# Moving opening angles to ScalarE, row copies to VectorE, weight stores to another queue, and re-slotting V in a tuned FNet and gMLP kernel

## The chip, the cores and the metric

The kernel runs on one core of one Trainium2 chip. The metric is device time in microseconds (us), lower is better; each figure is a median over several executions. Profiled spans are some 1 to 2 us shorter than the timed figure of the same execution, and a profile is one execution, so I compare profiles with profiles and times with times.

## The reference, cut to what matters

```python
X = np.fft.fft(np.fft.fft(x, axis=1), axis=2).real      # x: (8, 3072, 256)
h = np.maximum(X @ w_in, 0.0)                           # w_in: (256, 1024)
u, v = h[..., :512], h[..., 512:]
v_n = (v - mean(v)) / np.sqrt(var(v) + 1e-6)            # over the 512 columns
v_s = np.einsum('ts,bsd->btd', w_spatial, v_n) + b_spatial[None, :, None]
out = (u * v_s) @ w_out                                 # w_spatial: (3072, 3072)
```

The costly part is the spatial product: a 3072 x 3072 matrix on 3072 x 512 values, eight times.

## The kernel before

TensorE does everything that is a product, in bf16. Each batch's spatial product is cut in four *chunks* (c = 0 to 3). I number the chunks of batch 0 as chunks 0 to 3 and those of batch 1 as 4 to 7. Batches 0 and 1 use a 2 x 2 block scheme of eight products ("classic"). Batches 2 to 7 use a seven-product scheme ("fast") on weight sums such as A11 + A12, formed once on VectorE during batch 1, and on sums of V blocks, formed at each batch's start.

While a chunk's products run, the work that prepares later chunks is dropped into *slots* between them: folding x (the symmetry step ahead of the transform), transforms, V of the next batch, u of the next chunk, output products and, in batch 0, the turning (transposing) of the weights.

```python
def fold_steps(b, j, home=XHOME):          # pair(0), pair(1), c, d, e, g
    def pair(h):
        def go():
            bk = fbank()
            for i in range(2):              # mirrored rows of x through TensorE
                mm(bk[...], rid[...], view(mt, ...), True, True)
            xa = ev(512 * h, [1, 512])      # x itself, in the home's fp32 half
            tt(DVE, ov(512 * h, [1, 512]), xa, bk, SUB)
            tt(DVE, xa, xa, bk, ADD)
        return go
    ...                                     # the rest folds in place, in xt and oto

# batch 0
for c in range(4):
    ...                                     # folds, V of batch 1, turned tiles
    fillers(sl, n, ns, ((), ((0, 0, 7), (1, 7, 14)), ((2, 0, 13),), ((3, 0, 13),))[c])
    ...
    classic_chunk(0, n, c, units, sl, c == 0)

# batch 1: 15 weight sums a chunk, in thirds of a tile
sums = [...]                                # tt(DVE, o, A.., A..), then GpSimd stores o
sl.spread(sums, 0.6, 15.5)
...
# batches 2 to 7
if c == 0:
    for i, k in enumerate((0, 1, 2, 4, 6)):
        sl.at[k].append(vsum[i])            # M3, M4, M1, M6, M7: sums of V blocks
fillers(sl, n, 14, ((c, 0, 13),))           # V of the next batch, class c
```

A line `(c, lo, hi)` for `fillers` says which class of V is made between which slots. In these traces an instruction that waits holds up what the program put behind it on the same engine.

## Time and profile before

| what | before |
|---|---|
| time, median of 3 runs | 1398.86 us (1395.82 to 1401.41) |
| span of the profiled run | 1394.5 us |
| V of batch 0 starts (here: the first weight product of batch 0) | 73.5 us |
| chunks 0, 1, 2, 3 | 52.5, 65.1, 53.9, 47.9 us |
| chunk 7 with the gap behind it | 52.0 us (41.7 of work, 10.3 of gap) |
| first chunk of batch 2; of batches 3 to 6 | 46.1; 42.7, 43.7, 42.6, 43.7 us |
| other chunks of batches 2 to 5 | 36.2 to 36.4 us |

The chunk lengths come from the trace: a chunk begins with the first of its weight products on TensorE and ends where the next begins. For chunk 0 my cut falls on the product before its first one, so every length of chunk 0 is 0.4 to 0.5 us too long. The way to read this table is to hold it against the 36.2 us of an undisturbed fast chunk. The first chunk of a batch does the same products and takes 6 to 7 us more. In batch 0 the chunks have different work, so each has to be compared with its own busy TensorE time. The lines that carry this are in the prediction.

### The profile page before, as it was taken

The page shows a single profiled execution, that of the slowest core. Times are in us where ns is not written, and L with a number is a line of the kernel's source. Part 1 is how long each engine was busy: PE and PEld are TensorE (multiplying, and loading weights), DVE is VectorE, ACT ScalarE, POOL GpSimd, SP SyncE. Part 2 cuts the span into 40 slices and gives each one's busy share as a digit, 9 for nine tenths or more (in the row PEclk, how much of TensorE's full clock was granted, in tenths as well). Part 3 has the DMA queues.
Part 4 walks back from the last instruction along what each step waited for, and adds up shares of the span by engine and source line. Part 5 has one row for each costly group of instructions (what it writes and reads, how often), then busy time and mean ns, then how long its engine had stood idle before and what let it go on. Part 6 is the DMA issues. An engine that isn't in the chain of part 4 may idle for free.

```text
span 1394.5 us, 20891 instructions
## 1 busy us (share of the span) xinstructions
PE 1260.9 (90%) x8056; PEld 770.9 (55%) x8056; DVE 772.1 (55%) x1538; ACT 671.3 (48%) x1489; POOL 315.2 (23%) x372
## 2 busy tenths in 40 slices
PE   1685778999999978999899989999899989999998
PEld 0343445665665535665566655665566646666665
DVE  8676333534577743667555564557466654446333
ACT  4481266754445524555555545555455545552111
POOL 6322222310222211222222211222122222222222
PEclk9999899999999989999999999999999999999999
DMA  8646668778777775888678886888688767778885
GB/s 152 140 90 162 161 167 188 182 197 319 287 261 291 288 268 212 287 295 285 231 261 289 289 270 227 284 284 286 232 283 285 275 212 275 275 268 288 305 296 203
DMA packets 100435, 343.53 MB, mean 246 GB/s; under 512 B 10692, under 2 KB 60400, under 8 KB 74736
## 3 DMA queue, kind: packets, MB, share of 16 engines
q1 hardware_dynamic: 49424, 267.48, 53.8%
q0 software_dynamic: 25312, 49.55, 16.3%
q10 hardware_dynamic: 25600, 25.17, 5.3%
q8 instruction: 63, 1.03, 0.3%
q14 instruction: 36, 0.29, 0.1%
HBM read 300.46 MB, written 67.66 MB: 264 GB/s over the span
## 4 chain that ended last, share of the span: by engine, by line
PE 74%; DVE 9%; DMA 6%; ACT 5%; issue 2%; POOL 2%; SPq 0%; ACTq 0%; DVEq 0%; POOLq 0%
PE bk L115 72%; DMA reg<-rawd 2%; DVE reg L154 2%; PE bk L600 2%; DVE u L154 1%; ACT junk L422 1%; DVE y L154 1%; DMA reg<-sumd 1%; DMA ovl<-in_moe_w_spatial_dram 1%; ACT reg L607 1%; ACT reg L438 1%; DVE oto L154 1%; DMA xmr<-in_x_dram 1%; DVE ovl L154 1%; DMA qt<-in_moe_b_spatial_dram 1%
## 5 line engine op out<-in xcount | busy, mean ns | idle before, releaser
L115 PE MATMUL bk<-reg 128*128 128x384 bf16 (+1 forms) x5576 | 996.9, 330 | 37.6 <-DVE reg L154 19.4
L115 PEld LDWEIGHTS <-reg 128*128 128x128 bf16 x5576 | 546.4, 99 | 430.8 <-issue 64.1
L154 POOL TENSOR_TENSOR p<-y,qt 128x384 f32<-128x384 f32 x48 | 63.0, 1313 | 559.3 <-DVE y L154 559.3
L552 ACT COPY ost<-bk 128x512 f32<-128x512 f32 (+1 forms) x128 | 61.1, 479 | 246.5 <-PE bk L115 230.8
L438 ACT ACTIVATE reg<-vt,sm 128x512 bf16<-128x512 f32 x168 | 127.5, 807 | 76.0 <-DVE sm L154 48.7
L154 DVE TENSOR_TENSOR u<-y,u 128x384 bf16<-128x384 f32 x256 | 145.4, 568 | 9.6
L422 ACT ACTIVATE junk<-vt,sm 128x512 bf16<-128x512 f32 x168 | 121.3, 722 | 39.0 <-DVE sm L416 24.2
L154 DVE TENSOR_TENSOR y<-bk,bias 128x384 f32<-128x384 f32 x160 | 88.5, 553 | 92.7 <-PE bk L115 91.7
L533 ACT ACTIVATE u<-bk 128x384 bf16<-128x384 f32 x128 | 61.8, 483 | 87.9 <-PE bk L115 87.9
L115 PE MATMUL bk<-wob,u 128*128 128x256 bf16 x768 | 100.5, 273 | 0.2 <-ACT ost L552 0.2
L154 DVE TENSOR_TENSOR qt<-qt,bk 128x384 f32<-128x384 f32 x48 | 26.6, 554 | 126.9 <-PE bk L115 126.9
L527 ACT ACTIVATE u<-bk 128x384 bf16<-128x384 f32 x128 | 61.0, 476 | 59.5 <-PE bk L115 59.5
L115 PEld LDWEIGHTS <-u 128*128 128x128 bf16 x768 | 75.1, 98 | 19.9 <-DVE u L154 0.4
L154 POOL TENSOR_TENSOR qt<-y,qt 128x384 f32<-128x384 f32 x48 | 62.6, 1304 | 73.9 <-DVE y L154 69.3
L416 DVE TENSOR_SCALAR sm<-sm 128x2 f32<-128x2 f32 x84 | 33.9, 404 | 78.3 <-ACT vt L414 78.0
L154 DVE TENSOR_TENSOR ovl<-reg 128x1536 bf16<-128x1536 bf16 x60 | 56.6, 952 | 21.1 <-DMA reg<-rawd 12.5
L401 ACT ACTIVATE vt<-bk 128x512 f32<-128x512 f32 x84 | 49.7, 592 | 37.1 <-PE bk L115 37.1
L154 DVE TENSOR_TENSOR qt<-bias,bk 128x384 f32<-128x384 f32 x48 | 26.6, 554 | 73.7 <-PE bk L115 73.7
L115 PE MATMUL bk<-B,w2d 128*128 128x384 bf16 (+1 forms) x128 | 42.7, 334 | 26.7 <-ACT u L527 26.7
L154 DVE TENSOR_TENSOR reg<-reg 128x3072 bf16<-128x3072 bf16 (+2 forms) x34 | 66.4, 1954 | 0.1
L583 POOL COPY reg<-ovl 128x1535 bf16<-128x1535 bf16 x21 | 32.0, 1523 | 150.0 <-DMA ovl<-in_moe_w_spatial_dram 150.0
L922 POOL DMA_DIRECT2D sumd<-ovl x60 | 32.5, 542 | 146.2 <-DVE ovl L154 133.9
(132 smaller groups left out, 1324.9 us busy)
## 6 DMA issues: line engine op xcount, KB each, us to landing
reg<-sumd SPq DMA_DIRECT2D x120, 1152.0 KB
reg<-rawd SPq DMA_DIRECT2D x64, 1152.0 KB
out_dram<-ost ACTq DMA_DIRECT2D x64, 384.0 KB
sumd<-ovl POOLq DMA_DIRECT2D x60, 384.0 KB, 4.0
rawd<-reg SPq DMA_DIRECT2D x16, 1152.0 KB
bias<-bprm SPq DMA_DIRECT2D x32, 576.0 KB
ovl<-in_moe_w_spatial_dram POOLq DMA_DIRECT2D x45, 384.0 KB, 6.1
xst<-in_x_dram SPq DMA_DIRECT2D x22, 512.0 KB
```

The source lines that it names most:

```text
L115: PE.matmul(o, lhsT=l, rhs=r, start=start, stop=stop, skip_group_check=True)
L154: eng.tensor_tensor(out=o, in0=a, in1=b_, op=op)
L401: ACT.activation(out=v, in_=bk, func=AF.Relu, accum_out=sm[:, 0:1])
L416: DVE.tensor_scalar(out=sm[:, 2:4], in0=sm[:, 0:2], scalar1=-1.0 / DH, scalar2=None, op0=MUL)
L422: ACT.activation(out=junk, in_=s["v%d" % i], func=AF.Square, bias=sm[:, 2 + i:3 + i], accum_out=sm[:, 4 + i:5 + i])
L438: ACT.activation(out=o, in_=view(v, 0, [[256, 2], [1, 256]]), func=AF.Identity, scale=sm[:, 6 + i:7 + i], bias=sm[:, 8 + i:9 + i])
L527: ACT.activation(out=u[:, jc, 0, :], in_=src, func=AF.Relu)
L533: ACT.activation(out=u[:, jc, 1, :], in_=src, func=AF.Relu)
L552: ACT.copy(out=s["o"][:, rs[0]:rs[0] + len(rs), :], in_=view(bk, 0, [[256, len(rs)], [1, 256]]))
L583: POOL.tensor_copy(out=view(reg, ro + 1, [[1, 1535]]), in_=view(st, so + 1535, [[-1, 1535]]))
L600: PE.transpose(bk[:, 128 * n:128 * n + 128], view(src, off, [[4, 128]]), idn)
L922: POOL.dma_start(out=sumd[c, mi][:, 1536 * r:1536 * r + 1536], in_=o)
```

## The change

The intent is to take waiting out of the opening, batch 0, the step from batch 1 to 2, and each batch's first chunk. The diff, cut to its core:

```diff
+    def turns_of(c):                       # opening angles: twelve of these
+            ACT.activation(out=o, in_=..., func=AF.Identity, scale=sc, bias=bi)
...
     def mirror_rows(i, stage=None):        # reversed row copies
-        POOL.tensor_copy(out=view(reg, ro + 1, [[1, 1535]]),
+        DVE.tensor_copy(out=view(reg, ro + 1, [[1, 1535]]),
                         in_=view(st, so + 1535, [[-1, 1535]]))
...
+    def after_turn(i):                     # rows loaded and mirrored ahead
+        mirror_rows(i + 2)
+        load_part(i + 4, 1)
+        load_part(i + 3, 0)
...
-                    SP.dma_start(out=rawd[tc_, 2 * th + i],
+                    ACT.dma_start(out=rawd[tc_, 2 * th + i],
...                                         # batch 0: folds and V over more slots
-            for j in range(3):             # chunk 0 had all three folds of batch 1
+            fold_of(1, 0, 0, 3)
+            fold_of(1, 1, 4, 8)
+        elif c == 1:
+            fold_of(1, 2, 0, 4)
+        elif c == 2:
+            fold_of(2, 0, 8, 14)
+        else:
+            fold_of(2, 1, 2, 8)
+            fold_of(2, 2, 9, 15)
-        fillers(..., ((), ((0, 0, 7), (1, 7, 14)), ((2, 0, 13),), ((3, 0, 13),))[c])
+        fillers(..., ((), ((0, 4, 14),), ((1, 0, 6.5), (2, 6.5, 14)), ((3, 0, 11),))[c])
...                                         # chunk 7: sums early, first loads early
-        sl.spread(sums, 0.6, 15.5)
+        sl.spread(sums, 0.6, 15.5 if c < 3 else 8.0)
+        if c == 3:
+            load_next()
+            sl.at[8].append(load_next)
...                                         # first chunk of batches 2 to 7
-                for i, k in enumerate((0, 1, 2, 4, 6)):
+                for i, k in enumerate((0, 1, 2, 3, 4)):
-            fillers(sl, n, 14, ((c, 0, 13),))
+            fillers(sl, n, 14, ((c, 1 if c == 0 else 0, 13.5 if c == 0 else 13),))
```

The rest of the diff reorders the opening (the width tables come after the last angle tables, the turned tiles ahead of the third fold) and moves a scratch area.

More of the change, by code (lines that the diff above doesn't have):

```diff
@@ L214 @@
     F_TAB, F_WID, H_XST, H_HIS, F_SPX, H_SPC, H_WI, H_CT = (
-        0, 5072, 12800, 18944, 12288, 46208, 43008, 45056)
+        0, 19200, 12800, 18944, 12288, 46208, 43008, 45056)
     def special_load():
@@ L248, in table_ramps @@
                   channel_multiplier=3, allow_small_or_imprecise_dtypes=True)
-    def tables(c):
-        kv = view(regf, F_TAB, [[1, 385]])
-        yy = view(regf, F_TAB + 416, [[1, 1155]])
-        ta = view(regf, F_TAB + 1584, [[1, 1155]])
-        fv = view(regf, F_TAB + 2752 + 1160 * (c % 2), [[1, 1155]])
-        if c == 0:
-            DVE.tensor_scalar(out=view(regf, F_TAB + 404, [[1, 3]]),
-                              in0=view(regf, F_TAB + 400, [[1, 3]]),
-                              scalar1=1.0 / 3072.0, scalar2=None, op0=MUL)
-        for j in range(3):
-            DVE.tensor_scalar(out=view(regf, F_TAB + 416 + 385 * j, [[1, 385]]), in0=kv,
-                              scalar1=float(FREQ[c]),
-                              scalar2=view(regf, F_TAB + 404 + j, [[1, 1]]),
-                              op0=ADD, op1=MUL)
+        for i, f in enumerate((1, 2, 3)):
+            DVE.tensor_scalar(out=view(regf, F_TAB + 400 + 3 * i, [[1, 3]]),
+                              in0=view(regf, F_TAB + 400, [[1, 3]]),
+                              scalar1=(1.0 / 3072.0 if i == 0 else float(f)), scalar2=None,
+                              op0=MUL)
+    def turns_of(c):
+        for j in range(3):
+            o = view(regf, F_TAB + 416 + 1160 * (c % 2) + 385 * j, [[1, 385]])
+            sc = view(regf, F_TAB + 400 + j, [[1, 1]])
+            f = FREQ[c]
+            bi = 0.0 if f == 0 else view(regf, F_TAB + 400 + 3 * (f - 1) + j, [[1, 1]])
+            ACT.activation(out=o, in_=view(regf, F_TAB, [[1, 385]]), func=AF.Identity,
+                           scale=sc, bias=bi)
+    def tables(c):
+        yy = view(regf, F_TAB + 416 + 1160 * (c % 2), [[1, 1155]])
+        ta = view(regf, F_TAB + 2736, [[1, 1155]])
+        fv = view(regf, F_TAB + 3896 + 1160 * (c % 2), [[1, 1155]])
         DVE.tensor_scalar(out=ta, in0=yy, scalar1=MAGIC, scalar2=None, op0=ADD)
@@ L568, in u_ap, with load_part, mirror_rows @@
         return view(reg, WOFF[k] + 128 * t, [[1536, 3], [1, 128]])
-    def load_rows(i, stage=(ovl, 0)):
+    HST = ((ovl, 0), (reg, 32256))
+    def load_part(i, hi, stage=None):
+        if i >= 24:
+            return
         c, h, r = i // 6, i % 6 // 3, i % 3
         row = (TROW[c][h] + 512 * r) * S
-        POOL.dma_start(out=view(ovl, 1536 + 1536 * (i % 3), [[1, 1536]]),
-                       in_=dram(moe_w_spatial, row, [[4 * S, P], [1, 1536]]))
-        POOL.dma_start(out=view(stage[0], stage[1], [[1, 1536]]),
-                       in_=dram(moe_w_spatial, row + 1536, [[4 * S, P], [1, 1536]]))
-    def mirror_rows(i, stage=(ovl, 0)):
-        ro = 29184 + 1536 * (i % 3)
-        st, so = stage
-        POOL.tensor_copy(out=view(reg, ro + 1, [[1, 1535]]),
-                         in_=view(st, so + 1535, [[-1, 1535]]))
-        POOL.tensor_copy(out=view(reg, ro, [[1, 1]]), in_=view(st, so, [[1, 1]]))
+        t, o = (stage or HST[i % 2]) if hi else (ovl, 1536 + 1536 * (i % 3))
+        POOL.dma_start(out=view(t, o, [[1, 1536]]),
+                       in_=dram(moe_w_spatial, row + 1536 * hi, [[4 * S, P], [1, 1536]]))
+    def mirror_rows(i, stage=None):
+        if i >= 24:
+            return
+        ro = 29184 + 1536 * (i % 2)
+        st, so = stage or HST[i % 2]
+        DVE.tensor_copy(out=view(reg, ro + 1, [[1, 1535]]),
+                        in_=view(st, so + 1535, [[-1, 1535]]))
+        DVE.tensor_copy(out=view(reg, ro, [[1, 1]]), in_=view(st, so, [[1, 1]]))
+    def after_turn(i):
+        mirror_rows(i + 2)
+        load_part(i + 4, 1)
+        load_part(i + 3, 0)
     def turn_steps(i, k0, k1, on_dve=(1,)):
         r = i % 3
-        wo, ro = 1536 + 1536 * (i % 3), 29184 + 1536 * (i % 3)
+        wo, ro = 1536 + 1536 * (i % 3), 29184 + 1536 * (i % 2)
         steps = []
@@ L648 @@
     prep_x(0, 0)
+    turns_of(0)
+    turns_of(1)
     POOL.iota(view(regf, F_WID + 920, [[1, P]]), pattern=[[1, P]], base=1 - P,
@@ L661 @@
     for i in range(3):
-        load_rows(i, stages[i])
+        load_part(i, 0)
+        load_part(i, 1, stages[i])
     tables(0)
     tables(1)
+    turns_of(2)
+    turns_of(3)
     special_rows()
+    POOL.iota(view(regf, F_WID + 1060, [[1, P]]), pattern=[[1, P]], base=0,
+              channel_multiplier=-1, allow_small_or_imprecise_dtypes=True)
+    POOL.tensor_scalar(out=idn, in0=view(regf, F_WID + 1060, [[1, P]]), scalar1=0.0,
+                       scalar2=None, op0=ALU.is_equal)
     for f in fold:
@@ L669 @@
         s()
-    POOL.iota(view(regf, F_WID + 1060, [[1, P]]), pattern=[[1, P]], base=0,
-              channel_multiplier=-1, allow_small_or_imprecise_dtypes=True)
-    POOL.tensor_scalar(out=idn, in0=view(regf, F_WID + 1060, [[1, P]]), scalar1=0.0,
-                       scalar2=None, op0=ALU.is_equal)
-    width_tables()
     tables(2)
     tables(3)
+    width_tables()
+    load_part(3, 1)
+    load_part(4, 1)
+    POOL.dma_start(out=wob, in_=dram(moe_w_out, 0, [[D, P], [P * D, 4], [1, D]]))
+    width_products()
     for s in fold_steps(0, 1, homes[1]):
         s()
-    width_products()
+    mirror_rows(0, stages[0])
+    mirror_rows(1, stages[1])
+    for i in range(3):
+        for s in turn_steps(i, 0, 1, ()):
+            s()
+        if i == 0:
+            mirror_rows(2, stages[2])
+            load_part(3, 0)
+        else:
+            after_turn(i)
+    for k in range(2):
+        ACT.dma_start(out=rawd[0, k], in_=view(reg, WOFF[k], [[1, 4608]]))
     for s in fold_steps(0, 2, homes[2]):
         s()
-    POOL.dma_start(out=wob, in_=dram(moe_w_out, 0, [[D, P], [P * D, 4], [1, D]]))
     bias_rows()
     prep_x(1, 0)
-    for i in range(3):
-        mirror_rows(i, stages[i])
-    turned = []
-    for i in range(3):
-        ts = turn_steps(i, 0, 1)
-        ts[-1] = (lambda g=ts[-1], i=i: (g(), load_rows(i + 3)))
-        if i < 2:
-            ts.append(lambda i=i: mirror_rows(i + 3))
-        turned += ts
-    turned.append(lambda: mirror_rows(5))
-    for k, s in enumerate(turned):
-        s()
-    for k in range(2):
-        SP.dma_start(out=rawd[0, k], in_=view(reg, WOFF[k], [[1, 4608]]))
     load_bias(0)
@@ L723 @@
         tsi = turn_steps(i, 2, 3)
-        tsi[-1] = (lambda g=tsi[-1], i=i: (g(), load_rows(i + 3), mirror_rows(i + 3)))
+        tsi[-1] = (lambda g=tsi[-1], i=i: (g(), after_turn(i)))
         ts += tsi
@@ L738 @@
     for k in (2, 3):
-        SP.dma_start(out=rawd[0, k], in_=view(reg, WOFF[k], [[1, 4608]]))
+        ACT.dma_start(out=rawd[0, k], in_=view(reg, WOFF[k], [[1, 4608]]))
     def classic_chunk(b, n, c, units, sl, done=False):
@@ L858, with fold_of @@
         sl = Slots(ns)
-        if c == 0:
-            for j in range(3):
-                fs = fold_steps(1, j)
-                if j < 2:
-                    fs[-1] = (lambda g=fs[-1], j=j: (g(), prep_x(1, j + 1)))
-                else:
-                    fs[-1] = (lambda g=fs[-1]: (g(), prep_x(2, 0)))
-                sl.spread(fs, 2.5 * j, 2.5 * j + 3)
-        else:
-            j = c - 1
-            fs = fold_steps(2, j)
-            fs[-1] = (lambda g=fs[-1], j=j: (g(), prep_x(2, j + 1) if j < 2 else prep_x(3, 0)))
-            sl.spread(fs, 6, 14)
-        fillers(sl, n, ns, ((), ((0, 0, 7), (1, 7, 14)), ((2, 0, 13),), ((3, 0, 13),))[c])
+        def fold_of(fb, j, lo, hi):
+            fs = fold_steps(fb, j)
+            nb, nj = (fb, j + 1) if j < 2 else (fb + 1, 0)
+            fs[-1] = (lambda g=fs[-1]: (g(), prep_x(nb, nj)))
+            sl.spread(fs, lo, hi)
+        if c == 0:
+            fold_of(1, 0, 0, 3)
[4 more added lines that the diff above has]
+            fold_of(2, 0, 8, 14)
+        else:
+            fold_of(2, 1, 2, 8)
+            fold_of(2, 2, 9, 15)
+        fillers(sl, n, ns, ((), ((0, 4, 14),), ((1, 0, 6.5), (2, 6.5, 14)), ((3, 0, 11),))[c])
         seq = ([(c, 1)] if c > 0 else []) + ([(c + 1, 0)] if c < 3 else [])
@@ L880 @@
                 ts = turn_steps(ti, ua, ub)
-                if ti + 3 < 24:
-                    ts[-1] = (lambda g=ts[-1], ti=ti: (g(), load_rows(ti + 3),
-                                                       mirror_rows(ti + 3)))
+                ts[-1] = (lambda g=ts[-1], ti=ti: (g(), after_turn(ti)))
                 st += ts
@@ L896, with load_next @@
         classic_chunk(0, n, c, units, sl, c == 0)
+    seq = [(b, c, mi) for b in range(2, B) for c in range(4) for mi in range(7)]
+    pos = [0]
+    def load_next():
+        if pos[0] < len(seq):
+            b, c, mi = seq[pos[0]]
+            wload((pos[0] + 1) % 3, c, ORDER[mi])
+            pos[0] += 1
     cur = [0, 1, 4, 2]
@@ L938 @@
             cur = nxt
-    seq = [(b, c, mi) for b in range(2, B) for c in range(4) for mi in range(7)]
-    pos = [0]
-    def load_next():
-        if pos[0] < len(seq):
-            b, c, mi = seq[pos[0]]
-            wload(pos[0] % 3, c, ORDER[mi])
-            pos[0] += 1
-    for _ in range(3):
-        load_next()
+    load_next()
     g = 0
@@ L973 @@
                 sl.at[7].insert(0, lambda n=n: load_bias(n + 1))
-            units = [(g + i) % 3 for i in range(7)]
+            units = [(g + i + 1) % 3 for i in range(7)]
             g += 7
```

## The prediction

> **What bounds the kernel now.** I read the page first: busy time by engine and the chain that ended last.
>
> ```profile
> PE 1260.9 (90%) x8056; PEld 770.9 (55%) x8056; DVE 772.1 (55%) x1538; ACT 671.3 (48%) x1489; POOL 315.2 (23%) x372
> ...
> PE 74%; DVE 9%; DMA 6%; ACT 5%; issue 2%; POOL 2%; SPq 0%; ACTq 0%; DVEq 0%; POOLq 0%
> ```
>
> TensorE carries the chain and no other engine is near full, so a gain can only come from TensorE's idle time: 1394.5 - 1260.9 = 133.6 us. The second view is a table of stretches that I cut at the kernel's own stages, found from where each chunk's first products start: V of batch 0, then the four chunks of batch 0, the gap between batches 1 and 2, and one later batch. The columns are length, busy time of PE, PEld, DVE, ACT and POOL, granted clock, DMA share and GB/s.
>
> ```profile
> 60.80:106.50 45.70, 36.83 (x252) 21.42 (x252) 30.04 (x90) 36.70 (x70) 10.71 (x16) 1.00 0.58 136
> 106.50:158.60 52.10, 28.55 (x192) 18.02 (x192) 26.66 (x56) 8.63 (x13) 10.85 (x14) 0.80 0.59 130
> 158.60:226.50 67.90, 56.78 (x429) 35.56 (x427) 28.85 (x69) 46.33 (x96) 18.68 (x27) 0.98 0.72 179
> 226.50:279.00 52.50, 49.60 (x398) 33.41 (x398) 20.49 (x46) 31.11 (x59) 13.33 (x20) 0.99 0.85 204
> 279.00:327.00 48.00, 45.16 (x327) 29.09 (x325) 18.17 (x43) 25.32 (x53) 6.56 (x9) 1.00 0.81 241
> 489.00:500.00 11.00, 0.66 (x3) 0.32 (x4) 2.67 (x4) 0.47 (x1) 1.28 (x3) 0.71 1.02 330
> 529.00:682.00 153.00, 148.28 (x912) 89.57 (x911) 90.76 (x180) 79.60 (x189) 31.59 (x29) 0.98 0.80 269
> ```
>
> The idle time sits in chunk 0 of batch 0 (23.6 us), chunk 1 (11.1), the gap (10.3), and some 4.7 us once in each later batch. The timeline tells the cause of each. In chunk 0 TensorE waits twice for the mirrored x rows of a fold:
>
> ```profile
> 119.16 0.75 POOL L149 DMA_DIRECT2D xmr<-in_x_dram  x1
> 125.20 0.61 PE L115 MATMUL bk<-xmr,rid 128*128 128x256 bf16 x2 [7.72 <-DMA xmr<-in_x_dram]
> 143.92 0.75 POOL L149 DMA_DIRECT2D xmr<-in_x_dram  x1
> 148.07 1.03 PE L115 MATMUL bk<-xmr,rid 128*128 128x256 bf16 x4 [11.19 <-DMA xmr<-in_x_dram]
> ```
>
> GpSimd issues those loads in its own order, behind a row copy that itself waits for a transfer. The waits show that this is the rule: 21 copies, 150 us.
>
> ```profile
> POOL reg L583 <- DMA ovl<-in_moe_w_spatial_dram: 150.0, 21, 12.4
> ```
>
> Before batch 2 the first summed weights are asked for only when batch 1 has ended, and TensorE stands until they land:
>
> ```profile
> 491.76 1.13 SPq L830 DMA_DIRECT2D reg<-sumd  x2
> ...
> 499.34 4.02 PE L115 MATMUL bk<-reg 128*128 128x384 bf16 x12 [10.40 <-DMA reg<-sumd]
> ```
>
> In the first chunk of a batch the fifth sum of V runs late on VectorE; ScalarE's normalised V of the next batch overwrites what that sum reads, so ScalarE waits, the u activation behind it waits, and TensorE with it:
>
> ```profile
> 676.46 2.55 DVE L154 TENSOR_TENSOR reg<-reg 128x3072 bf16<-128x3072 bf16 x1
> ...
> 679.04 1.52 ACT L438 ACTIVATE reg<-vt,sm 128x512 bf16<-128x512 f32 x2 [5.29 <-DVE reg L154]
> ...
> 681.56 0.48 PE L115 MATMUL bk<-B,w2d 128*128 128x384 bf16 x1 [4.41 <-ACT u L527]
> ...
> 681.83 3.59 PE L115 MATMUL bk<-reg 128*128 128x384 bf16 x12
> ```
>
> The same 4.41 us stands at 528.7, 833.1, 985.7 and 1137.0 us: five times, never in the last batch, which prepares no next V.
>
> [...] twelve products take 3.59 us after the wait and 2.11 us elsewhere. [...] the fold's 128x508 addition takes 0.69 us alone and 1.51 us beside the GpSimd copy.
>
> **The change, part by part.**
>
> *Angles on ScalarE.* Twelve VectorE multiplies of 385 elements (458 ns each, 5.5 us counted singly) become twelve ScalarE activations of about 0.5 to 0.7 us (estimate: a 385-wide ScalarE cast takes 0.48 us, and an activation with two per-partition operands costs more). At the start nothing comes of it: the first fold waits until 9.5 us for its rows anyway. Later tables 2 and 3 need 2 x (0.76 + 1.36) = 4.2 us of VectorE instead of 6.4. But the width tables now follow them, and GpSimd's ramps for these stand behind a memset that waits for ScalarE's sine of table 3: I place the width tables at 28 us, the width products at 31 to 37, the second fold (6.2 us) until about 42. The three turned tiles come before the third fold: nine ScalarE copies at 1.01 us plus the first latency, to about 53.5, and the third fold, 6.2 us, to about 60, where before it ended at 51.9 and the turning at 58.2. First transforms: 1 to 2 us later.
>
> *Copies on VectorE, three tiles ahead.* GpSimd loses 24 x (1.5 + 0.2) = 41 us and all its waits for landing; VectorE gains 24 x about 0.7 = 17 us [...]. In chunk 0 VectorE has 12.4 us for two folds, 8.8 for eight gates (0.55 + 0.56 each), 2 for turned copies, 2.1 for mirrors: 25 us. The mirrored x rows are issued early, as TensorE alone reads them. The other half of x still loads when the fold before has ended, some 5 us, now with one such wait inside chunk 0 because the third fold moves to chunk 1. TensorE's own work there is about 25 us at full clock. Chunk 0: about 28 us instead of 52.1.
>
> *V over more slots.* One V chunk (about 3.5 us of TensorE and 16 of ScalarE) leaves chunk 1, and chunk 2 takes one more. Chunk 1: 56.8 - 3.5 + 5 of waits for the third fold = 58.5 (was 67.9). Chunk 2: 49.6 + 3.5 + 7, as ScalarE there has 31 + 17 us to do = 60 (was 52.5). Chunk 3 gets a second fold: 48.5 (was 48.0). The four chunks: 195 instead of 220.5, so -25.5; with the opening -24.
>
> *Stores on ScalarE's queue.* 16 issues at about 0.4 us, off the path; the sync queue no longer stands behind them (86.9 us of waits), which no TensorE wait rests on. Zero.
>
> *First loads for batch 2, sums done by slot 8.* Saved: 10.4 us of standing, 1.9 on twelve products at half clock, 0.4 on transforms: 12.7. Given back: 15 sums at 0.95 us now meet folds, V and gates in eight slots (some 27 us of VectorE in 21), so chunk 7 may lose 3. Net -9.5.
>
> *V sums in slots 0 to 4, next V one slot later.* The last sum then starts at about 671.0 where the fourth did, ends at 673.6, and ScalarE first needs it after 677. VectorE's queue stays even: the fourth sum fits the 2 us before 669.9 when it waited for TensorE. Saved at each of five boundaries: 4.41 + 3.70 - 2.11 (cold against warm products) = 6.0; together -30.
>
> Sum: -24 - 9.5 - 30 = -63.5; 1398.9 - 63.5 = 1335, and I say 1336.
>
> **Rivals.** (a) *The waits in batch 0 only move.* For: the x load still follows the fold before, ScalarE has 48 us of work in chunk 2, and DMA is at 0.85 there. Against: DMA demand there is fixed at 0.85 x 52.5 = 45 us a chunk. Then only 5 of 24 us come: about 1355. (b) *The reversed copy is slow on VectorE.* [...] (c) *VectorE becomes the bound at the batch boundary* and the 4.41 us wait becomes one for a bank. For: five sums at 1.75 to 2.55 us in five slots of 2.45. Against: the count above. Half of the 30 lost: 1351. (d) *Better than I say:* the earlier stream also frees the opening, where GpSimd doubles VectorE's times, and chunk 2 stays near its TensorE time: 1322.
>
> **Range and chances.** The boundary and the gap, 40 us, are read from waits that repeat to 0.01 us; batch 0 carries the doubt, +-15. Predicted 1336, range 1318 to 1360. Faster by over 2% means below 1370.9, which the 40 us alone pass: 0.93. Within 2%: 0.06. Slower: 0.01.
>
> **What would show it.** Right: five waits of 4.41 us gone and a batch of about 147 us; no idle at the start of batch 2; chunk 0 below 32 us with no wait on mirrored x; the VectorE copy near 0.56 us. Wrong: a TensorE wait on ScalarE copies or VectorE in chunks 1 and 2 that restores their 120 us; first transforms later than 63 us; waits on summed weights in batch 2.

## The result, and the profile after

The changed kernel takes 1352.85 us (median of 4 runs, 1350.76 to 1354.26) beside 1397.34 us for the kernel before (median of 4). The ratio is 0.9676, with a 95% interval of 0.965 to 0.9703. A ratio, here and below, is the mean time of one kernel's runs over that of the other's of the same rounds, so it is not quite the ratio of the medians. Executions over 1.5% slower than the fastest of the same kernel are left out of the means.

It is faster by 3.2%, and 17 us above the point predicted. Most places that the prediction named changed, several of them not by the amounts given. First the page, busy time by engine and the chain that ended last:

```profile
PE 1248.3 (92%) x7995; PEld 767.5 (57%) x8056; DVE 765.6 (57%) x1573; ACT 682.4 (51%) x1505; POOL 271.7 (20%) x324
...
PE 72%; issue 9%; DVE 6%; ACT 5%; DMA 4%; POOL 2%; another core or an unknown queue 0%; ACTq 0%; POOLq 0%; DVEq 0%
```

TensorE's idle time fell from 133.6 to 1350.6 - 1248.3 = 102.3 us. Its busy time fell too, by 12.6 us, for the same work: fewer products ran cold, as I call the lower granted clock behind a wait (in the kernel before 0.50 over the 4.0 us behind the wait of 10.40 us, where twelve products took 4.02 us beside 2.11 elsewhere; over the whole span 0.978 before and 0.982 after), and the trace holds 61 products fewer, as some records can be missing. The views do not part the two. Now the same table of stretches, cut at the starts of this kernel's own stages: V of batch 0, chunks 0 to 3, chunk 7, and one batch from its second chunk to the next batch's first. The columns are those of the prediction's table.

```profile
60.80:106.40 45.60, 36.71 (x248) 21.51 (x252) 30.74 (x96) 36.66 (x70) 3.23 (x6) 0.98 0.45 108
106.40:134.10 27.70, 24.59 (x191) 16.28 (x189) 21.37 (x46) 8.56 (x13) 3.61 (x6) 0.94 0.87 214
134.10:198.50 64.40, 52.43 (x399) 34.13 (x399) 26.26 (x70) 30.97 (x60) 7.67 (x14) 0.92 0.78 194
198.50:264.80 66.30, 55.61 (x415) 36.11 (x417) 25.13 (x67) 43.52 (x92) 7.08 (x13) 0.95 0.71 176
264.80:315.90 51.10, 45.52 (x331) 29.27 (x332) 25.41 (x64) 28.13 (x56) 2.60 (x4) 1.00 0.59 201
437.50:490.80 53.30, 45.21 (x253) 26.28 (x253) 31.23 (x59) 19.91 (x47) 10.57 (x20) 0.90 0.80 288
527.40:672.70 145.30, 144.56 (x903) 88.35 (x910) 89.64 (x179) 79.39 (x189) 31.56 (x28) 1.00 0.83 283
```

The last line is the clean one: in a whole batch TensorE is idle for 0.7 us. About half of what is left lies where the change gained nothing: 43.6 us of idle TensorE ahead of 60.8 us, where the kernel before had 43.1, and 8.9 us in the first line, as before. The other losses sit in four lines. Chunk 1 has 12.0 us of idle TensorE, chunk 2 has 10.7, chunk 3 has 5.6 and chunk 7 has 8.1, and three of the four show a granted clock below 1.00. The granted clock is what to look at beside the idle time: the 12 us of chunk 1 cost more than 12, since the products after the long wait run slowly: over the 4.2 us behind it the granted clock is 0.50, and the first twelve weight products there take 3.45 us where 2.11 is usual.

| length in us | before | after | change |
|---|---|---|---|
| start of V of batch 0 | 73.5 | 73.8 | +0.3 |
| chunk 0 | 52.5 | 27.6 | -24.9 |
| chunk 1 | 65.1 | 64.5 | -0.6 |
| chunk 2 | 53.9 | 66.3 | +12.4 |
| chunk 3 | 47.9 | 51.1 | +3.2 |
| chunk 7 and the gap | 52.0 | 53.3 | +1.3 |
| first chunk of batch 2 | 46.1 | 36.5 | -9.6 |
| first chunks of batches 3 to 6 | 172.7 | 146.0 | -26.7 |

These add up to -44.6; the spans differ by 43.9. What TensorE waited for in chunks 1, 2 and 7 says where to look. The columns of the waits are the instruction that waited, what released it, us in total, times, and the longest. Chunk 1 of the kernel after:

```profile
PE bk L115 <- DVE xst L154: 9.8, 1, 9.8
```

Chunk 2 of the kernel after:

```profile
PE bk L115 <- ACT vt L407: 6.7, 3, 3.0
PE bk L616 <- ACT reg L623: 3.0, 1, 3.0
```

Chunk 7 of the kernel after:

```profile
PE bk L115 <- ACT u L533: 3.6, 1, 3.6
PE bk L115 <- DVE y L154: 2.3, 1, 2.3
PE bk L115 <- ACT vt L420: 1.3, 1, 1.3
```

The kernel before had no such waits in these chunks: in chunk 1 none for x beyond 0.7 us, in chunk 2 none over 1.2 us, in chunk 7 a single one of 1.0 us. Chunk 1's own waits of old, 10.1 us for turned copies, u and V, shrank to 1.4. After the 2.3 us in chunk 7 twelve products took 4.00 us where 2.11 is usual, at a granted clock of 0.50. Followed back in the timeline, the 9.8 us of chunk 1 end in a transfer. These lines, from three engines' timelines, have start, length, what was done, and in brackets the idle time ahead of it and what ended it:

```profile
135.35 0.81 ACTq L910 DMA_DIRECT2D rawd<-reg  x2
...
136.56 0.38 SPq L141 DMA_DIRECT2D xst<-in_x_dram  x1
...
147.75 0.69 DVE L154 TENSOR_TENSOR oto<-xst,bk 128x512 f32<-128x512 f32 x1 [10.29 <-DMA xst<-in_x_dram]
...
149.22 0.59 PE L115 MATMUL bk<-xmr,rid 128*128 128x256 bf16 x2 [9.79 <-DVE xst L154]
```

ScalarE's queue asks for the stores of two turned tiles (2 x 128 x 4608 x 2 bytes = 2.4 MB). Then 1.2 us later the sync queue asks for the x of the third fold (0.5 MB), which VectorE can use only 11.2 us after that. The prediction had put some 5 us there.

In the first chunk of batches 3 to 6 the wait of 4.41 us is gone; no wait of TensorE over 1 us is left between 527 and 690 us. The reversed copy on VectorE took 0.56 us:

```profile
42.18 0.56 DVE L594 COPY reg<-reg 128x1535 bf16<-128x1535 bf16 x1
```

### The profile page after: what moved, and what is told of

The parts are those of the page before. It is cut to its first block, busy times and chain, and to the rows that moved or that the text cites.

```text
span 1350.6 us, 20874 instructions
## 1 busy us (share of the span) xinstructions
PE 1248.3 (92%) x7995; PEld 767.5 (57%) x8056; DVE 765.6 (57%) x1573; ACT 682.4 (51%) x1505; POOL 271.7 (20%) x324
## 4 chain that ended last, share of the span: by engine, by line
PE 72%; issue 9%; DVE 6%; ACT 5%; DMA 4%; POOL 2%; another core or an unknown queue 0%; ACTq 0%; POOLq 0%; DVEq 0%
PE bk L115 70%; POOL sumd L953 2%; PE bk L616 2%; DMA reg<-sumd 1%; ACT junk L428 1%; DMA xst<-in_x_dram 1%; DMA xmr<-in_x_dram 1%; DVE xst L154 1%; DVE oto L154 1%; DVE u L154 1%; ACT reg L623 1%; DVE y L154 1%; DMA sumd<-ovl 0%; DVE ovl L154 0%; ACT reg L473 0%
## 5 line engine op out<-in xcount | busy, mean ns | idle before, releaser
L115 PE MATMUL bk<-reg 128*128 128x384 bf16 (+1 forms) x5576 | 988.4, 329 | 27.6 <-ACT reg L309 20.6
L558 ACT COPY ost<-bk 128x512 f32<-128x512 f32 (+1 forms) x128 | 61.1, 479 | 269.9 <-PE bk L115 248.0
L539 ACT ACTIVATE u<-bk 128x384 bf16<-128x384 f32 x128 | 61.6, 482 | 66.3 <-PE bk L115 66.2
L533 ACT ACTIVATE u<-bk 128x384 bf16<-128x384 f32 x128 | 61.1, 477 | 54.2 <-PE bk L115 54.2
L407 ACT ACTIVATE vt<-bk 128x512 f32<-128x512 f32 x84 | 49.7, 591 | 32.0 <-PE bk L115 31.9
L420 ACT ACTIVATE vt<-bk 128x512 f32<-128x512 f32 x84 | 49.1, 584 | 27.9 <-PE bk L115 27.9
L422 DVE TENSOR_SCALAR sm<-sm 128x2 f32<-128x2 f32 x84 | 32.4, 386 | 52.1 <-ACT vt L420 51.3
L154 POOL TENSOR_TENSOR p<-p,y 128x384 f32<-128x384 f32 x48 | 47.7, 995 | 59.3 <-DVE y L825 38.6
L623 ACT COPY reg<-bk 128x1024 bf16<-128x1024 bf16 x51 | 50.9, 1011 | 17.3 <-PE bk L616 17.1
```

The lines of the kernel that those rows point to most:

```text
L115: PE.matmul(o, lhsT=l, rhs=r, start=start, stop=stop, skip_group_check=True)
L154: eng.tensor_tensor(out=o, in0=a, in1=b_, op=op)
L407: ACT.activation(out=v, in_=bk, func=AF.Relu, accum_out=sm[:, 0:1])
L420: ACT.activation(out=v, in_=bk, func=AF.Relu, accum_out=sm[:, 1:2])
L422: DVE.tensor_scalar(out=sm[:, 2:4], in0=sm[:, 0:2], scalar1=-1.0 / DH, scalar2=None, op0=MUL)
L533: ACT.activation(out=u[:, jc, 0, :], in_=src, func=AF.Relu)
```

## The experiments

My theory after this reading had three parts. Chunk 7 loses what the early loads gain, as fifteen sums crowd VectorE's queue. Chunk 1 loses to the late x. Chunk 2 loses to ScalarE, which has two classes of V there. Rivals were that the early load itself delays chunk 7, and that batch 0 is bound by its transfers, so that waits only move. Twelve kernels ran; all gave the reference's result. Experiments 5, 6, 10 and 11 ran on another chip than the other eight. Each ratio is to the kernel before, and is to be held against the 0.9676 of the kernel after.

Chunk lengths come from one profile each. In the kernel after and in experiments 1, 2, 5, 6 and 9, which leave the chunks of batch 0 as they are, chunk 0 takes 26.0 to 27.8 us, chunk 1 63.9 to 64.5, chunk 2 66.2 to 68.3 and chunk 3 51.1 to 52.7, the four together 209.5 to 211. Differences of 2 us in one of these chunks are no finding.

### 1. Sums over the whole of chunk 7

```diff
-        sl.spread(sums, 0.6, 15.5 if c < 3 else 8.0)
+        sl.spread(sums, 0.6, 15.5)
-        for mi, (ka, kb, op) in (...):                  # order 2, 1, 0, 3, 4
+        for mi in (2, 1, 0, 3, 4) if c < 3 else (2, 4, 0, 1, 3):
```

> The kernel after, with the fifteen weight sums of chunk 7 (the last chunk of batch 1) spread over the whole chunk again, the two groups that read the tile which the second early load overwrites coming first; both early loads stay. Chunk 7 takes 53.3 us in the kernel after, and had 41.7 us of its own in the kernel before. Theory 'crowding' (fifteen sums in eight slots make gates and V statistics queue on VectorE): chunk 7 falls to 42 to 45 us and the time from 1352.9 to about 1343. Rival 'early load' (the 1.2 MB asked for at the start of chunk 7 share the transfer engines with the two tiles that the sums wait for): chunk 7 stays above 51 us, the time above 1350.

Measured: 1339.87 us, ratio 0.9591 (0.9577 to 0.9605). Chunk 7 takes 41.8 us, with the early loads in it and no gap behind it. Its line in the table of stretches:

```profile
437.70:479.50 41.80, 40.22 (x254) 24.77 (x254) 28.60 (x56) 19.92 (x47) 8.86 (x17) 1.00 0.91 335
```

The transfer share is higher than in the kernel after (0.91 against 0.80) and the chunk is 11.5 us shorter, with the clock back at 1.00. This speaks for crowding and against the early load. The order of the sums changed with their spread, because the second early load overwrites what two groups read; the run does not part the two.

### 2. Sums still crowded, no early loads

```diff
-        if c == 3:
-            load_next()
-            sl.at[8].append(load_next)
...
-    load_next()
+    for _ in range(3):
+        load_next()
```

> The kernel after with the sums still crowded into the first eight slots of chunk 7, but with all three first loads for batch 2 asked for after chunk 7, as before. Theory 'crowding': chunk 7's own work stays at 51 to 53 us and the gap of about 10 us before batch 2 comes back on top: about 1364. Rival 'early load': chunk 7's own work falls to 42 to 45 us and the gap comes back, so the two cancel: about 1353.

Measured: 1357.19 us, ratio 0.9716 (0.9701 to 0.973). Chunk 7 and the gap take 58.7 us, of which TensorE stands 5.9 us for the first summed weights, so the chunk's own work stays at 52.8. That is what crowding predicts. The gap that came back is smaller than the 10 us I expected:

```profile
PE bk L115 <- DMA reg<-sumd: 5.9, 1, 5.9
```

The loads were asked for at 489.2 us, as TensorE's last product ran. The kernel before asked 2.8 us after its chunk's end, because the request stood 2.7 us behind VectorE's last sum. So crowding costs the chunk 11 us with or without early loads. With crowded sums the early loads are worth 4 to 7 us (4 to 6 by the times, 7 by the chunks); with the sums spread, experiment 1 shows the whole gap of 10.3 us gone. They never needed the crowding.

What crowding means can be read from VectorE's own waits in chunk 7 of the kernel after:

```profile
DVE ovl L154 <- DMA reg<-rawd: 5.1, 1, 5.1
DVE ovl L154 <- DMA sumd<-ovl: 3.1, 3, 1.8
```

A sum stands for the load of a tile that it reads, and others for the stores of earlier sums. In the kernel before these waits were 2.2 us and nothing, in this experiment they are 5.4 and 1.1. So sums that come early wait for their data, early loads or not, and hold up the gates and statistics behind them.

### 3. The x of batch 1's third fold asked for early

```diff
+    XEARLY = ((regf, 9728), (reg, 21504))       # space that V of batch 1 takes later
+    prep_x(1, 2, XEARLY)                        # ahead of chunk 0
...
-            fs = fold_steps(fb, j)
+            fs = fold_steps(fb, j, XEARLY if (fb, j) == (1, 2) else XHOME)
...                                             # x of batch 2's first fold is asked for one fold earlier
```

> The kernel after, but the x rows of batch 1's third fold get a home of their own and are asked for at the start of chunk 0, not when the second fold has ended. In the kernel after chunk 1 takes 64.5 us and TensorE stands 9.8 us in it, as x takes 11 us to land behind the stores and tile loads. Theory 'late x' (that wait and the cold clock after it are chunk 1's loss): chunk 1 falls to 51 to 54 us, chunk 0 stays at 27 to 29, the time goes from 1352.9 to about 1341. Rival 'transfers at their limit' (the same bytes only compete elsewhere): chunk 1 stays above 60 us or chunk 0 or 2 grows by what it loses, and the time stays above 1349.

Measured: 1340.19 us, ratio 0.9598 (0.9582 to 0.9614). Chunk 0 takes 26.0 us, chunk 1 takes 52.1, chunk 2 takes 67.9. Chunk 1 in the table of stretches:

```profile
133.00:185.10 52.10, 49.73 (x399) 32.83 (x399) 26.21 (x70) 31.00 (x60) 6.36 (x12) 1.00 0.89 225
```

The same 399 products take 49.73 us of busy TensorE where they took 52.43, and idle time falls from 12.0 to 2.4 us. So chunk 1's loss was 9.6 us of waiting and 2.7 us of cold products (granted clock 0.92 over the chunk there, 1.00 here). The transfers run at a share of 0.89 and the waits do not reappear elsewhere: the four chunks together are 12.8 us shorter. So batch 0 was not at the limit of its transfers.

### 4. V of batch 1 spread from chunk 2 into chunk 3

```diff
-  ((1, 0, 6.5), (2, 6.5, 14)), ((3, 0, 11),)
+  ((1, 0, 8),), ((3, 4, 13),)       # class 2: chunk 2 slots 8 to 16, chunk 3 slots 0 to 4
```

> The kernel after, but the V work of batch 1 in chunk 2 is spread thinner: one class in slots 0 to 8, the first half of the next in slots 8 to 16, its second half in the first four slots of chunk 3, and the last class in slots 4 to 13 there (it was two classes in chunk 2 and one in chunk 3). Chunk 2 takes 66.3 us and chunk 3 51.1 in the kernel after. Theory 'ScalarE fills chunk 2' (43.5 us of its work in two long runs make TensorE wait for V and turned tiles): chunk 2 falls to 56 to 59 us, chunk 3 rises to 53 to 56, the time goes to about 1347. Rival 'folds and turned copies on VectorE, or transfers, bound chunk 2': chunks 2 and 3 together stay within 2 us of their 117.4 and so does the time.

Measured: 1357.02 us, ratio 0.9716 (0.9698 to 0.9733). Chunk 2 fell to 59.8 us, near what I expected, but chunk 3 rose to 63.7. It is a miss for both theories, and its trace says why. TensorE's longest wait in chunk 3 was for u:

```profile
PE bk L115 <- ACT u L539: 5.2, 1, 5.2
```

ScalarE's u activation stood behind a normalisation that needed a reciprocal from VectorE, and VectorE stood behind x:

```profile
299.45 0.69 DVE L154 TENSOR_TENSOR oto<-xst,bk 128x512 f32<-128x512 f32 x1 [8.03 <-DMA xst<-in_x_dram]
300.17 0.69 DVE L154 TENSOR_TENSOR xst<-xst,bk 128x512 f32<-128x512 f32 x1
300.77 0.16 DVE L435 RECIPROCAL sm<-sm 128x2 f32<-128x2 f32 x1
```

```profile
301.16 1.52 ACT L444 ACTIVATE reg<-vt,sm 128x512 bf16<-128x512 f32 x2 [5.46 <-DVE sm L154]
```

The reciprocal, 0.16 us of work, waited for an x load that it has nothing to do with. It is chunk 1's fault once more, in the chunk that has two folds: an x load asked for (at 290.97 us) in the chunk that needs it. In the kernel after VectorE's wait for this load was 3.6 us, and TensorE waited for nothing over 2.4 us in that chunk.

### 5 and 6. The batch boundary, one half at a time

Experiment 5 keeps the V sums in slots 0 to 4 and puts the next V back to slots 0 to 13:

```diff
-            fillers(sl, n, 14, ((c, 1 if c == 0 else 0, 13.5 if c == 0 else 13),))
+            fillers(sl, n, 14, ((c, 0, 13),))
```

> The kernel after, but with only one half of the batch-boundary part: the five sums of V stay in slots 0 to 4, and the next batch's V goes back to slots 0 to 13 (it was one slot later). First chunks of batches 3 to 6 take 36.5 us in the kernel after and 42.6 to 43.7 in the kernel before. Theory 'the last sum was late' (what counts is that it ends before ScalarE overwrites what it reads; it now ends some 5 us earlier): chunks stay at 36.5 to 37.5, time within 3 us of 1352.9. Rival 'both halves are needed' (ScalarE's first normalised V comes a slot sooner too and still meets the sum): 38.5 us or more each, 1363 or more.

Measured: 1358.73 us, ratio 0.9726 (0.9704 to 0.9748); the first chunks of batches 2 to 6 take 37.6 us each. Experiment 6 keeps V later and puts the sums back:

```diff
-                for i, k in enumerate((0, 1, 2, 3, 4)):
+                for i, k in enumerate((0, 1, 2, 4, 6)):
```

> The kernel after with only the other half: the next batch's V one slot later, the sums of V back in slots 0, 1, 2, 4 and 6. Theory 'the last sum was late': the wait of 4.41 us shrinks by one slot of some 2.45 us to about 2[...], so first chunks take 38 to 39.5 us and the time is 1361 to 1368. Rival 'the delay of V alone suffices': 36.5 us and 1353.

Measured: 1360.72 us, ratio 0.9747 (0.9723 to 0.977); these chunks take 38.2 us each. With batches 3 to 6 at 43.2 on average before and 36.5 after, the sums alone bring 5.6 of 6.7 us and the later V alone 5.0. They do not add because both shorten the same wait. TensorE's wait of 4.41 us in the kernel before brought cold products behind it (in batch 3 twelve took 3.59 us beside 2.11 elsewhere, and the granted clock was 0.57 over 3.8 us); either half alone makes it 0.9 or 1.4 us, and these chunks are 1.1 or 1.7 us longer than in the kernel after, so little is left for the other half. In the first chunk of batch 3, for experiment 5 and then for experiment 6:

```profile
PE bk L115 <- ACT u L533: 0.9, 1, 0.9
```

```profile
PE bk L115 <- ACT u L539: 1.4, 1, 1.4
```

Against what was expected, the chunks of experiment 5 lie just outside the theory's range (37.5) and its time is 5.9 us up, where 3 were allowed; five boundaries at 1.1 us account for it. Experiment 6 is as the theory has it in its chunks and 0.3 us under its range in time.

### 7. Stores back on the sync queue

```diff
-            ACT.dma_start(out=rawd[...], ...)    # in all three places
+            SP.dma_start(out=rawd[...], ...)
```

> The kernel after with the stores of turned weight back on the sync queue. The prediction: zero, so 1351 to 1355. Rival 'order of the queue': the x rows of a fold are asked for in the same slot just ahead of the stores, so on one queue they would go ahead of the 2.3 MB and land sooner than the 11 us of the kernel after: chunk 1 falls from 64.5 to 58 to 61 us and the time to 1347 to 1350. Rival 'the sync queue blocks': x loads and loads of summed weights wait behind stores that wait for turned copies: chunks 1 to 3 grow and the time passes 1357.

Measured: 1345.38 us, ratio 0.9619 (0.9599 to 0.9638). Chunk 1 takes 56.8 us instead of 64.5. The sync queue's and VectorE's timelines of this kernel:

```profile
137.09 0.38 SPq L141 DMA_DIRECT2D xst<-in_x_dram  x1
137.57 0.93 SPq L910 DMA_DIRECT2D rawd<-reg  x2
```

```profile
141.40 0.69 DVE L154 TENSOR_TENSOR oto<-xst,bk 128x512 f32<-128x512 f32 x1 [3.41 <-DMA xst<-in_x_dram]
```

Now x is asked for 0.5 us ahead of the stores, and VectorE can use it 4.3 us later instead of 11.2. So this part of the change was not free: it costs about 8 us by the ratios and 6.0 in the profiled spans (7.7 in chunk 1, with 2.9 given back in chunks 2 and 3). In chunk 1 it let the 2.4 MB be asked for first. Whether the one queue or only the earlier request makes x land sooner, this run does not tell apart.

### 8. Row copies back on GpSimd, rows still three tiles ahead

```diff
-        DVE.tensor_copy(out=view(reg, ro + 1, [[1, 1535]]), ...)
+        POOL.tensor_copy(out=view(reg, ro + 1, [[1, 1535]]), ...)
```

> The kernel after with the reversed row copies back on GpSimd, in the same place of the program, so with the rows still loaded three tiles ahead. Theory 'the look-ahead did it' (GpSimd's waits of 12.4 us each for landing rows held up the mirrored x loads; with rows loaded ahead they are gone, whoever copies): chunk 0 stays below 30 us and the time within 4 us of 1352.9. Rival 'the engine did it' (a copy of 1.5 us or more on GpSimd, its queue ahead of the x loads, and VectorE slowed beside it): chunk 0 above 33 us or chunks 1 to 3 longer by 10 us in sum, and 1363 or more.

Measured: 1357.98 us, ratio 0.9716 (0.9692 to 0.974). V of batch 0 starts 1.9 us earlier, chunk 0 takes 26.0 us, and chunks 1, 2 and 3 take 65.3, 70.8 and 54.2. A copy costs 1.50 us on GpSimd. So chunk 0 does not need VectorE for its gain: the look-ahead and the fold moved out of it are enough (these two I did not part). The four chunks together are 6 to 7 us longer than in the kernels with the same batch 0 (216.3 against 209.5 to 211), most of it in chunks 2 and 3, so the engine is worth that, less the 1.9 us that the opening gains by GpSimd. That VectorE's copy of 0.56 us feeds the turning sooner is the likely reason; it is not shown. Each theory has a part: by time, 5.1 us up, the first missed its 4 us and the rival's 1363 was not reached.

### 9. Opening angles back on VectorE

```diff
-            ACT.activation(out=o, in_=..., func=AF.Identity, scale=sc, bias=bi)
+            DVE.tensor_scalar(out=o, in0=..., scalar1=sc, scalar2=bi, op0=MUL, op1=ADD)
```

> The kernel after with the twelve opening angles back on VectorE (one multiply and add of 385 elements each), everything else as it is. The prediction gave the change of the opening +1 to +2 us in all and put none of it down as a gain of the angles: 1351 to 1353, V of batch 0 starting within 1 us of 73.8. Rival 'ScalarE took load off VectorE when it counts': V starts 2 to 5 us later, 1355 to 1358. Rival 'the angles cost more than they gave' (they bring a third table load of 1.28 us and about 0.6 us each on ScalarE): V starts 2 us or more earlier, 1350 or less.

Measured: 1351.92 us, ratio 0.967 (0.965 to 0.9691): the same time. In its profile V starts at 76.4 us, where the ten kernels with the opening of the kernel after, that one included, gave 73.4 to 75.2, so the angles may be worth 1 to 3 us of the opening. The time shows none of it; chunk 0 is 1.6 us shorter here, but it takes either 26.0 or 27.3 to 27.8 us from run to run in kernels that do not touch it. The third table load that one rival counts is there: the kernel after loads ScalarE's tables at 0.75, 5.49 and 66.14 us, 1.28 us each, the kernel before at 0.74 and 65.80. I leave this part as "no measurable effect".

### 10. A version with 1 and 3, and one fold to a chunk

```diff
+        elif c == 1: fold_of(1, 2, 0, 4); fold_of(2, 0, 8, 14)
+        elif c == 2: fold_of(2, 1, 8, 14)
+        else:        fold_of(2, 2, 7, 14)
```

> A version meant to beat both: sums of chunk 7 spread over the chunk and x of batch 1's third fold asked for early, as in the two runs that measured 13 us and 12.7 us less; and as the x loads are now a chunk ahead, the folds of batch 2 stand one in each of chunks 1, 2 and 3 (they were one in chunk 2 and two in chunk 3), so that no x load is asked for in the chunk that needs it. If the two gains add: 1352.9 - 13.0 - 12.7 = 1327.2, and chunk 3 with one fold less takes 48 to 50 us where it had 51: 1325. Rival 'one gain hides the other or chunk 1 pays for its second fold': chunk 1 above 55 us, time above 1330.

Measured: 1327.03 us, ratio 0.9504 (0.9483 to 0.9526). Chunk 1 takes 53.2, chunk 2 takes 67.6, chunk 3 takes 48.9 and chunk 7 takes 41.6. The two gains add (1327.2 was the sum). The folds of batch 2 were moved in the same run; what that move is worth (2 us less in chunk 3, 1 more in chunk 1) lies within the spread of one profile, and it was not run by itself.

### 11. The same with V of batch 1 spread evenly

```diff
-  ((0, 4, 14),), ((1, 0, 6.5), (2, 6.5, 14)), ((3, 0, 11),)
+  ((0, 4, 11),), ((2, 4, 14),), ((3, 0, 11),)   # class 1: chunk 1 from slot 11, chunk 2 to slot 4
```

> The same version with V of batch 1 spread evenly: the second class in slots 11 to 16 of chunk 1 and 0 to 4 of chunk 2, the third in slots 4 to 14 of chunk 2 (chunk 2 had both). Theory 'two V classes on ScalarE make chunk 2 long' (TensorE waits there 10.1 us for ScalarE): chunk 2 falls from about 67 to 58 to 60 us and chunk 1 rises from 52 to 55 to 57, the time by about 5 us to 1320. Rival 'V costs the same wherever it stands': the two chunks together unchanged, and 1325.

Measured: 1325.9 us, ratio 0.9495 (0.9475 to 0.9514). Chunks 1 and 2 take 60.8 and 60.4 us, in sum 121.2 where they took 120.8: the rival's case, but for chunk 3, which is 2.5 us shorter. V on ScalarE costs the two chunks the same in these two placements, and the time (0.9495 against 0.9504) does not tell the versions apart. The waits of chunk 2 changed their name, from V to turned tiles:

```profile
PE bk L616 <- ACT reg L623: 6.1, 3, 2.6
```

### 12. The same with two of three turned copies on VectorE

```diff
-                ts = turn_steps(ti, ua, ub)
+                ts = turn_steps(ti, ua, ub, (0, 2))
```

> The even version (1325.9) with two of the three turned copies of each tile on VectorE and one on ScalarE in chunks 0 to 3 (it was the reverse). One costs 0.69 us on VectorE and 1.01 on ScalarE. Theory 'ScalarE is what chunk 2 waits for' (6.1 us of TensorE's waits there are for ScalarE's turned copies): chunk 2 falls from 60.4 to 55 to 57, chunk 1 from 60.8 to 58 to 60, the time to 1318 to 1321. Rival 'the wait changes its name': TensorE waits as long for VectorE's copies, 1325 or more.

Measured: 1322.77 us, ratio 0.9458 (0.9433 to 0.9482). Chunk 2 falls from 60.4 to 54.4 us and ScalarE's busy time there from 40.9 to 35.4; chunk 1 stays at 60.9. What TensorE waits for in chunk 2 is now spread thin, and its longest two waits are:

```profile
PE bk L115 <- ACT u L539: 1.6, 1, 1.6
PE bk L616 <- DVE reg L621: 1.2, 2, 0.9
```

So in chunk 2 it was ScalarE's load, not V as such. Chunk 1 did not follow, and the time is 1.8 us above the range expected. Nearly all of the gain is given back in this profile: chunk 0 takes 1.9 us more, and the third chunk of batch 1 takes 44.2 us where it took 41.2, with one wait of 2.3 us for u, behind a normalisation that waits 3.4 us for VectorE. That is why the profiled spans of experiments 11 and 12 (1321.6 and 1321.0 us) hardly differ and the intervals of their ratios touch; the gain in time is not shown. Both beat the kernel after clearly, by about 2% of the time before.

## Why the prediction was right or wrong

The class and the range were right: 1352.85 lies within 1318 to 1360, and the direction was never in doubt. The point was 17 us low. By its own steps, with the chunk lengths of the profiled runs:

- **Opening, +1 to +2.** Measured +0.3 at the start of V. Right in kind: no gain from the angles, which experiment 9 bears out. An activation took 0.67 us in the mean (0.60 to 0.61 for the three with one per-partition operand, 0.69 for the nine with two), within the 0.5 to 0.7 estimated. The places given inside it held: the second fold ended at 42.2 us (about 42 predicted) and the third at 58.4 (about 60).
- **Reversed copy, near 0.56 us.** Measured 0.545 to 0.565 us over 24 copies, and 0.15 for the one element copied behind each, 0.71 for the pair where about 0.7 was counted; on GpSimd the copy takes 1.50 us (experiment 8). The 0.56 was my estimate; no trace of the kernel before could show it, as that kernel has no such copy on VectorE. Rival (b) is out. One reading beside it was wrong: the addition of 1.51 us, which takes 0.69 elsewhere, ended at 45.24 us and GpSimd's copy began at 45.26, so it ran beside GpSimd's requests for transfers. The operations that did run beside the copies were slower too: one of 128x256 took 1.68 us there and 0.42 elsewhere.
- **Chunk 0, about 28 us.** Measured 27.6. The reason was right as well, and experiment 8 narrows it: chunk 0 is as short with GpSimd copying, so it was not the change of engine that freed the mirrored x loads.
- **Chunk 1, 58.5 us.** Measured 64.5; wrong by 6. The prediction's table ends chunk 1 at 226.5 us, where chunk 2's first product ran at 223.6, so the 67.9 and 56.8 that it starts from were 65.1 and 54.3 (and its terms add to 58.3). Started rightly the sum is 55.8, and the miss 8.7. The step that failed is "some 5 us" for the load of x. Behind the stores of this very change it took 11.2; TensorE stood 12.0 us in the chunk, and the wait brought 2.7 us of cold products (granted clock 0.92 in the chunk). Experiment 3 removes the wait: 52.1.
- **Stores, "Zero".** Wrong. The text asked whether a wait of TensorE rested on the *sync* queue's waits, and none did; it did not ask what the stores would be in front of on their new queue. Experiment 7 gives about 8 us back by undoing this part, and chunk 1 falls by 7.7: it is the miss of chunk 1 once more.
- **Chunk 2, 60 us.** Measured 66.3; wrong by 6. Cut at its own first products, the chunk before had 50.6 us of busy TensorE and not 49.6, which makes the sum 61.1. The rest is two terms: busy time came to 55.6 where 54.1 was counted, and 7 us for ScalarE's load was too little, as idle time is 10.7, 10.1 of it waits for ScalarE. The mechanism, ScalarE overfull in chunk 2, was right (experiment 12).
- **Chunk 3, 48.5 us.** Measured 51.1; it has two folds and an x load between them. With one fold it takes 48.9 (experiment 10).
- **Chunk 7 gives back 3 us.** The largest miss by the figures as given: it gave back 11.6 (53.3 against 41.7 us). The step counted VectorE's busy time, "some 27 us of VectorE in 21", and took the small excess for the whole cost. But the queue runs in order (0.16 us of work stood behind a wait of 8.03 us in experiment 4), and the early sums themselves waited for transfers (8.2 us where it was 2.2): gates and V's statistics stood behind sums, ScalarE behind the statistics, TensorE behind ScalarE, and the granted clock was 0.90 over the chunk. Experiment 1 takes all of it away without giving up the early loads.
- **Gap, 12.7 us saved.** The gap is gone, as predicted, and with it the cold products behind it (twelve took 4.02 us at a granted clock of 0.50). Experiment 2 adds what the step did not see: part of the old gap was a request that stood behind the last sum, and with the sums done early the gap is 5.9 us even without early loads.
- **Boundaries, 5 x 6.0 = 30 us.** Right (the sum's 3.70 for twelve cold products is no line of the trace; five groups took 3.44 to 4.05): four of them gave 26.7, or 6.7 each, and the fifth is in the -9.6 of batch 2's first chunk. The account of the cause, the last sum ending too late, held too, though experiments 5 and 6 show that either half of the edit would have brought five sixths or three quarters of it.

Of the rivals, (a) was half right: waits in batch 0 moved, from chunk 0 to chunks 1 and 2. It gave 1355 as the time, close to what came, but its reason, that too little would be gained in batch 0, was only part of it. Over chunks 0 to 3 the gain was 9.9 us, not 5, and the remaining miss lay in chunk 7. Batch 0 was also not bound by its transfers, as experiment 3 shows. (c) did not come: VectorE became no bound at the boundary. (d) did not come either, but the faster versions pass it by hand: 1322.77 us.

What stays open: experiment 12's loss in batch 1, and whether stores on the sync queue would still help the versions that ask for x early. These combinations were not run.

## What to carry to other kernels

A sum of busy times does not price work that is put into an in-order queue. Ask which small operation will stand behind it (here a reciprocal of 0.16 us that stood behind a wait of 8.03 us), and who waits for that one. Before a transfer is moved to another queue, ask what it will now be ahead of; a load on the critical path should be asked for a stage early, or at least ahead of bulk stores (here x could be used 4.3 us after a request ahead of 2.4 MB of stores on one queue, and 11.2 us after one behind them on two). And when a change is a bundle, look at each part by itself after it has won: here two parts of a good change cost 8 and 11 us.
